# A query sketch sent through DRAM and read back repeated, later loads ungated: polysketch attention followed by a squared-ReLU feed-forward

## The chip, the cores and the metric

The kernel runs on 1 core of one Trainium2 chip. The metric is device microseconds of one execution; a kernel's number is the median of its runs. Engines in the profiles: PE (matmuls), PEld (its weight loads), DVE (vector), ACT (scalar), POOL (GpSimd), SP (issues most transfers).

## The reference

```python
def phi(x):                                   # S1, S2: 8 x 32;  x: (4 batches, 4 heads, 1088, 32)
    a = np.einsum('rd,bhsd->bhsr', S1, x)     # first sketch
    b = np.einsum('rd,bhsd->bhsr', S2, x)     # second sketch
    return np.einsum('bhsi,bhsj->bhsij', a, b).reshape(*x.shape[:-1], 64)
q_p, k_p = phi(q), phi(k)
kv = np.einsum('bhsf,bhsd->bhfd', k_p, v)
z = np.sum(k_p, axis=2)
num = np.einsum('bhsf,bhfd->bhsd', q_p, kv)
den = np.einsum('bhsf,bhf->bhs', q_p, z)[..., None] + 1e-06
x = (num / den) as (4352 tokens, 128)
r = np.maximum(x @ w_in, 0.0)                 # w_in: 128 x 2048
out = (r * r) @ w_out                         # w_out: 2048 x 128
```

The work falls into attention, batch by batch, and the feed-forward in chunks of 512 tokens, which needs the attention of its tokens.

## The kernel before

At build time a small list scheduler inside the kernel puts some 600 operations in a fixed order on each engine, from a table of ranks and its own guesses of durations. At run time each engine works through its list and waits on semaphores. So an engine doesn't overtake its own list, even when something behind is ready (in early_no_trip below, POOL stood for 15.9 us before one product, with copies behind it).

The query path of batches 1 to 3. PE makes both sketches in repeated form (64 rows for the 8 x 8 pairs: one repeats its rows, the other tiles them), ACT copies one out of PSUM, DVE multiplies it with the other:

```python
for u, (base, n, xs_) in enumerate(((0, 256, (0, 1)), (512, 256, (0, 1)), (1024, 64, (0,))) if b else ...):
    def f_m(e, ...):
        for ab in range(2):                    # both sketches
            for x in xs_:
                for h in range(H):
                    ...
                    nc.tensor.matmul(at(hb[x])[64 * y : 64 * y + 64, c0 : c0 + n],
                        SR[32 * h : 32 * h + 32, ab].rearrange("p x y -> p (x y)"), rhs, start=True, stop=True)
    def f_ac(e, ...):
        nc.scalar.copy(at(sA)[:, 0 : 2 * n]..., src(ab=0))
    def f_qp(e, ...):
        nc.vector.tensor_tensor(out=o, in0=i0, in1=i1, op=ALU.mult)      # qp
```

The loads. POOL issues weights and the inputs of batches 1 to 3 in one chain, paced by landings three transfers back. The first waits for v of batch 0, and the loads of batches 2 and 3 wait for the first normalised output of the batch before:

```python
o_gate = add("gate", {"POOL": ...}, lambda e: nc.gpsimd.tensor_copy(gate[96:128], vin[0][96:128, H - 1, 7, D - 1 : D]), ...)
...
load_v(1, -35)
load_q(1, -34)
...
if b > 1:
    load_k(b, vt(0) - 30, hist[(b, "gate")])
    load_v(b, vt(0) - 29)
    load_q(b, vt(0) - 28)
...
def f_gt(e, db=db):
    nc.gpsimd.tensor_copy(gateb, at(db)[2][:, 0, 0:1])      # waits for xs of batch b
```

The denominators get epsilon on DVE (`nc.vector.tensor_scalar_add(dn_, v4[:, :, :, D], eps)`), then reciprocal, product (`xs`), transpose on PE (`xT`), feed-forward.

## Time and profile before

| | before |
|---|---|
| median, range of its first 3 runs | 119.99 us, 119.92 to 120.73 |
| span of the profiled run, mean clock of PE | 118.0 us, 0.995 |
| first denominators of batches 0 and 1 | 12.81, 37.32 us |

Columns: line, engine, operation, out<-in, shapes, count | busy us, mean ns | idle time of the engine just before, and what ended most of it.

```profile
L707 ACT ACTIVATE r<-h 128x1024 bf16<-128x1024 f32 x53 | 52.0, 1046 | 4.6 <-PE h L698 3.3
L698 PE MATMUL h<-xT,w_in 128*128 128x512 bf16 (+1 forms) x152 | 36.2, 348 | 1.0 <-ACT r L707 0.7
...
L717 DVE TENSOR_TENSOR g<-r 128x1024 bf16<-128x1024 bf16 x46 | 30.6, 698 | 0.7 <-ACT r L707 0.3
L715 ACT ACTIVATE g<-r 128x1024 bf16<-128x1024 bf16 x22 | 23.7, 1089 | 0.2
L709 DVE TENSOR_SCALAR r<-h 128x1024 bf16<-128x1024 f32 x15 | 18.0, 1210 | 1.1 <-PE h L698 1.1
...
L629 PE MATMUL h<-kvz,qp 128*64 128x66 f32 x288 | 10.4, 225 | 0.4 <-DVE kvz L553 0.2
```

Relu (`r`) and square (`g`) of the feed-forward take 52.0 + 23.7 us of ACT and 30.6 + 18.0 of DVE, 124.3 us, so 62 us for each of the two engines. PE's own part of the feed-forward is 272 matmuls of 512 columns at 0.215 us, 58.5 us.

### The profile page before, as it was taken

The page shows a single profiled execution, that of the slowest core. Times are in us where ns is not written, and L with a number is a line of the kernel's source. Part 1 is how long each engine was busy: PE and PEld are TensorE (multiplying, and loading weights), DVE is VectorE, ACT ScalarE, POOL GpSimd, SP SyncE. Part 2 cuts the span into 40 slices and gives each one's busy share as a digit, 9 for nine tenths or more (in the row PEclk, how much of TensorE's full clock was granted, in tenths as well). Part 3 has the DMA queues.
Part 4 walks back from the last instruction along what each step waited for, and adds up shares of the span by engine and source line. Part 5 has one row for each costly group of instructions (what it writes and reads, how often), then busy time and mean ns, then how long its engine had stood idle before and what let it go on. Part 6 is the DMA issues. An engine that isn't in the chain of part 4 may idle for free.

```text
span 118.0 us, 3582 instructions
## 1 busy us (share of the span) xinstructions
PE 108.2 (92%) x1442; PEld 66.6 (56%) x1460; DVE 96.6 (82%) x179; ACT 91.9 (78%) x140; POOL 30.5 (26%) x73
## 2 busy tenths in 40 slices
PE   5998999999999998999999999999899999999850
PEld 2377676665666653555757545447656544567640
DVE  2658579989959699997559999999679989999920
ACT  0542367699885799999997999998649999999910
POOL 6139165593000764600006643300000000000000
PEclk9999999999999999999999999999999999999998
DMA  3960968774210299200401948102200050040522
GB/s 107 291 170 6 154 169 126 105 200 183 37 16 6 62 292 232 73 6 10 74 11 23 298 82 235 24 12 39 48 0 0 3 89 8 6 81 3 89 45 45
DMA packets 22272, 10.19 MB, mean 86 GB/s; under 512 B 19008, under 2 KB 20672, under 8 KB 22256
## 3 DMA queue, kind: packets, MB, share of 16 engines
q0 software_dynamic: 2688, 6.06, 20.6%
q1 hardware_dynamic: 18560, 3.54, 15.1%
q10 hardware_dynamic: 1008, 0.36, 1.4%
q8 instruction: 11, 0.18, 0.7%
q14 instruction: 5, 0.04, 0.1%
HBM read 8.78 MB, written 2.23 MB: 93 GB/s over the span
## 4 chain that ended last, share of the span: by engine, by line
PE 53%; ACT 18%; DVE 12%; issue 8%; DMA 4%; POOL 2%; DVEq 0%; ACTq 0%
PE o L724 16%; PE h L698 15%; ACT r L707 10%; PE h L629 6%; PE o L325 5%; DMA kin<-in_k_dram 4%; DVE g L717 4%; ACT g L715 3%; PE a L538 3%; PE h L583 2%; DVE qp L609 2%; PE a L496 2%; ACT A L598 2%; PE h L496 2%; DVE kT L476 1%
## 5 line engine op out<-in xcount | busy, mean ns | idle before, releaser
L707 ACT ACTIVATE r<-h 128x1024 bf16<-128x1024 f32 x53 | 52.0, 1046 | 4.6 <-PE h L698 3.3
L698 PE MATMUL h<-xT,w_in 128*128 128x512 bf16 (+1 forms) x152 | 36.2, 348 | 1.0 <-ACT r L707 0.7
L724 PE MATMUL o<-g,w_out 128*128 128x512 bf16 (+1 forms) x154 | 33.7, 346 | 1.5 <-DVE osb L731 0.5
L717 DVE TENSOR_TENSOR g<-r 128x1024 bf16<-128x1024 bf16 x46 | 30.6, 698 | 0.7 <-ACT r L707 0.3
L715 ACT ACTIVATE g<-r 128x1024 bf16<-128x1024 bf16 x22 | 23.7, 1089 | 0.2
L698 PEld LDWEIGHTS <-w_in 128*128 128x128 bf16 x160 | 16.6, 115 | 12.6 <-issue 3.1
L724 PEld LDWEIGHTS <-w_out 128*128 128x128 bf16 x160 | 15.1, 98 | 13.4 <-issue 1.6
L709 DVE TENSOR_SCALAR r<-h 128x1024 bf16<-128x1024 f32 x15 | 18.0, 1210 | 1.1 <-PE h L698 1.1
L609 DVE TENSOR_TENSOR qp<-h,A 128x512 f32<-128x512 f32 (+2 forms) x22 | 11.9, 562 | 2.9 <-ACT A L598 2.8
L598 ACT COPY A<-h 128x512 f32<-128x512 f32 (+2 forms) x22 | 10.0, 504 | 4.7 <-PE h L583 4.6
L629 PEld LDWEIGHTS h<-kvz,qp 128*64 128x64 f32 x288 | 9.2, 137 | 3.7 <-DVE qp L609 2.0
L583 PE MATMUL h<-qT,SR 32*64 32x256 f32 (+2 forms) x352 | 10.8, 338 | 0.1
L629 PE MATMUL h<-kvz,qp 128*64 128x66 f32 x288 | 10.4, 225 | 0.4 <-DVE kvz L553 0.2
L325 PE MATMUL o<-wz 128*128 128x512 bf16 x26 | 8.6, 450 | 1.5 <-DVE mk L288 1.2
L538 PEld LDWEIGHTS a<-vp,kp 128*64 128x64 f32 x216 | 6.9, 138 | 2.8 <-issue 2.2
L583 PEld LDWEIGHTS h<-qT,SR 32*64 32x64 f32 x352 | 6.2, 131 | 3.1 <-ACT r L707 0.8
L538 PE MATMUL a<-vp,kp 128*64 128x33 f32 x216 | 7.6, 224 | 0.2
L731 DVE STREAM_TRANSPOSE osb<-o 128x512 f32<-128x512 f32 (+1 forms) x10 | 6.3, 629 | 1.4 <-PE o L724 1.4
L663 POOL COPY gateb<-xs 128x1 bf16<-128x1 bf16 x3 | 0.6, 189 | 25.3 <-DVE xs L652 25.3
L360 POOL DMA_DIRECT2D vin<-in_v_dram x12 | 6.6, 560 | 0.4 <-issue 0.4
L476 DVE STREAM_TRANSPOSE kT<-kin 128x512 f32<-128x512 f32 x8 | 5.3, 681 | 1.4 <-DMA kin<-in_k_dram 1.4
L521 DVE TENSOR_TENSOR kp<-a,ka 128x512 f32<-128x512 f32 (+1 forms) x8 | 5.9, 747 | 0.5 <-ACT kb L511 0.5
(65 smaller groups left out, 88.5 us busy)
## 6 DMA issues: line engine op xcount, KB each, us to landing
kin<-in_k_dram POOLq DMA_DIRECT2D x3, 544.0 KB, 5.1
qin<-in_q_dram POOLq DMA_DIRECT2D x3, 544.0 KB, 3.6
vin<-in_v_dram POOLq DMA_DIRECT2D x12, 128.0 KB, 4.5
out_dram<-osb SPq DMA_DIRECT2D x16, 64.0 KB, 1.9
w_in<-in_moe_w_in_dram POOLq DMA_DIRECT2D x4, 128.0 KB, 3.7
w_out<-in_moe_w_out_dram POOLq DMA_DIRECT2D x4, 128.0 KB, 3.9
qin<-in_q_dram SPq DMA_DIRECT2D x1, 416.0 KB
out_dram<-osb SPq DMA_DIRECT2D x10, 32.0 KB, 1.6
```

The source lines that it names most:

```text
L325: nc.tensor.matmul(tiles["o"][0][:, 0:512], wz[:, 0:128], wz, start=True, stop=True)
L538: nc.tensor.matmul(t[64 * (h % 2) : 64 * (h % 2) + 64, 33 * (h // 2) : 33 * (h // 2) + 33], kp[i][:, j, h, :], vp[i][:, h, j, :], start=(j ...
L583: nc.tensor.matmul(at(hb[x])[64 * y : 64 * y + 64, c0 : c0 + n], SR[32 * h : 32 * h + 32, ab].rearrange("p x y -> p (x y)"), rhs, start=Tr ...
L598: nc.scalar.copy(at(sA)[:, 0 : 2 * n].rearrange("p (r s) -> p r s", s=n), src(ab=0))
L609: nc.vector.tensor_tensor(out=o, in0=i0, in1=i1, op=ALU.mult)
L629: nc.tensor.matmul(at(nb)[64 * hf : 64 * hf + 64, col(x, pr)], qp[i][:, pr, n0 : n0 + 64], kvz[i][xx % 2][:, pr].rearrange("p y d -> p (y ...
L698: nc.tensor.matmul(at(hb)[:, step * w : step * w + N], w_in[:, 512 * (ct // E) : 512 * (ct // E) + 512].rearrange("p (c e) -> p e c", e=E) ...
L707: nc.scalar.activation(o, view(at(hb)), ACTF.Relu)
L709: nc.vector.tensor_scalar_max(o, view(at(hb)), 0.0)
L715: nc.scalar.activation(at(gb)[:, 0 : W * N], r, ACTF.Square)
L717: nc.vector.tensor_tensor(out=at(gb)[:, 0 : W * N], in0=r, in1=r, op=ALU.mult)
L724: nc.tensor.matmul(at(ob)[:, 0:N], w_out[:, ct, :], at(gb)[:, N * w : N * w + N], start=(ct == 0), stop=(ct == CT - 1))
```

## The change

The intent: take the repetition of one sketch off PE, and its copy off ACT. For batches 1 to 3, PE makes this sketch A compact (32 output rows a group), A is written to DRAM, and two transfers read it back repeated eight times into SBUF. The other sketch is made in tiles of 512 columns and multiplied by A from SBUF. The first gate goes from v to the first part of q of batch 0; batch 1's q is loaded ahead of its v; the loads of batches 2 and 3 have no gate of their own. Epsilon is added on ACT, key products are cut differently, and the order on all engines is new.

```diff
-        for u, (base, n, xs_) in enumerate(
-                ((0, 256, (0, 1)), (512, 256, (0, 1)), (1024, 64, (0,))) if b else ...
+        if b:
+            def f_A(e):
+                w = lambda x: SKD[:, x].rearrange("p r y c -> p (r y c)")
+                for g in range(4):
+                    nc.tensor.matmul(at(ab_)[32 * g : 32 * g + 32, 0:256], w(g // 2), qT[i][:, 256 * g : 256 * g + 256], ...)
+                ...
+            o_As = add(f"As{b}", {"ACT": act(272), "DVE": dve(272)}, ...)
+            o_aw = add(f"aw{b}", {"SP": (0.6, 3.0)}, lambda e: nc.sync.dma_start(
+                out=Aw[i].rearrange("r y j (g s) -> g (r y j) s", g=4), in_=As[i]), ...)
+            for pr in range(2):
+                def f_ar(e, pr=pr):
+                    nc.sync.dma_start(out=Ar[i][:, pr, :], in_=Aw[i][pr].rearrange("y j s -> (y j) s")[:, None, :].to_broadcast([16, R, S]))
+            def f_m(e):
+                ...                                  # one sketch, 8 matmuls of 512 columns
+            for x in range(2):
+                ...                                  # DVE: qp = sketch (PSUM) * Ar (SBUF), 1024 elements
...
-    o_gate = add("gate", ..., nc.gpsimd.tensor_copy(gate[96:128], vin[0][96:128, H - 1, 7, D - 1 : D]), ...)
+    o_gate = add("gate", ..., nc.gpsimd.tensor_copy(gate[96:128], qin[0][96:128, 0:1]), pri=-45)
...
-    load_v(1, -35)
-    load_q(1, -34)
+    load_q(1, -35)
+    load_v(1, -34)
...
-                load_k(b, vt(0) - 30, hist[(b, "gate")])
-                load_v(b, vt(0) - 29)
-                load_q(b, vt(0) - 28)
+                load_q(b, vt(0) - 30)
+                load_k(b, vt(0) - 29)
+                load_v(b, vt(0) - 28)
...
-                nc.vector.tensor_scalar_add(dn_, v4[:, :, :, D], eps)
+                    nc.scalar.activation(dn_, v4[:, :, :, D], ACTF.Identity, bias=epsT[:, 0:1])
```

## The prediction

> **What bounds the kernel now.** I read the page's busy table and slices first, then its chain that ended last, then the groups by line, and then the timeline in three places: the start, the query path of batch 1, and one later batch. The page of the kernel before gives, per engine, busy time, share of the span and instructions, and below it the busy tenths in 40 slices of 2.95 us:
>
> ```profile
> PE 108.2 (92%) x1442; PEld 66.6 (56%) x1460; DVE 96.6 (82%) x179; ACT 91.9 (78%) x140; POOL 30.5 (26%) x73
> ...
> PE   5998999999999998999999999999899999999850
> ...
> DVE  2658579989959699997559999999679989999920
> ACT  0542367699885799999997999998649999999910
> ...
> PE 53%; ACT 18%; DVE 12%; issue 8%; DMA 4%; POOL 2%; DVEq 0%; ACTq 0%
> ```
>
> The reader should see three engines near full, PE first, and PE as over half of the chain. DVE and ACT dip together in the first seven slices and near slices 12 to 14, 20 to 22 and 29 to 31. The last three dips are the query parts of batches 1 to 3. The groups concerned (busy us, mean ns of one):
>
> ```profile
> L724 PE MATMUL o<-g,w_out 128*128 128x512 bf16 (+1 forms) x154 | 33.7, 346 | 1.5 <-DVE osb L731 0.5
> ...
> L609 DVE TENSOR_TENSOR qp<-h,A 128x512 f32<-128x512 f32 (+2 forms) x22 | 11.9, 562 | 2.9 <-ACT A L598 2.8
> L598 ACT COPY A<-h 128x512 f32<-128x512 f32 (+2 forms) x22 | 10.0, 504 | 4.7 <-PE h L583 4.6
> ...
> L583 PE MATMUL h<-qT,SR 32*64 32x256 f32 (+2 forms) x352 | 10.8, 338 | 0.1
> ...
> L663 POOL COPY gateb<-xs 128x1 bf16<-128x1 bf16 x3 | 0.6, 189 | 25.3 <-DVE xs L652 25.3
> ```
>
> L583 makes both sketches of q, L598 copies one out of PSUM, L609 multiplies them: 4.6 us of ACT and 2.8 us of DVE go in waiting inside this hand-over. The gate's 25.3 us of POOL cost nothing by themselves, since POOL is 26% busy.
>
> Is PE really the bound? The timeline puts the first numerator's denominators of batches 1, 2 and 3 at 37.32, 61.72 and 85.68 us: a batch takes about 24.2 us. Four feed-forward matmuls of 512 columns take 0.86 us on the chain, so 0.215 each; a batch has 1088/512 x 32 = 68 of them, 14.6 us. Attention of batch 3, from the timeline: kv 1.13 + 1.36, key sketch 0.45 + 0.75 + 0.45, query sketch 1.12 + 1.12 + 0.46, numerator 1.16 + 1.39, transposes 0.39 + 0.52, in all 10.3 us, of which I estimate 1 us as overlap of pipeline ends with the next group. So PE has about 24 us of work in a 24.2 us batch: once running, it is bound by PE, with ACT and DVE some 10% short of full (between 40 and 66 us they were busy 24.27 and 21.83 of 26).
>
> The start is different. Until 40 us only 768 tokens (48 big-matmul equivalents of 512 columns, 10.3 us) and two attentions (some 19 us) are done. The lines of the start, from the timeline (start us, us, engine, what):
>
> ```profile
> 10.21 0.18 POOL L346 COPY gate<-vin 32x1 f32<-32x1 f32 x1
> ...
> 11.63 0.55 POOL L360 DMA_DIRECT2D kin<-in_k_dram  x1
> ...
> 25.20 0.56 POOL L360 DMA_DIRECT2D qin<-in_q_dram  x1
> ```
>
> Batch 1's keys are asked for at 11.6 us and used at 16.72, its queries asked for at 25.2 and used at 30.4, its last query product ends at 39.2. Meanwhile PE runs warm-up matmuls on zeros: 2.8 us of them after 15 us. So the start is bound by loads that are gated late.
>
> **What the Trainium skill says.** "TensorE: Matmul & The Clock Gate", section "Wait — 56ns, not 53.3ns?", gives 215.7 ns from start to start at N = 512 when warm; this trace's 0.215 us agrees, so nothing is to be had from the feed-forward matmuls. "TensorEngine Tiling (Array Packing)", "Key Properties": changing the tiling mode drains TensorE; the trace shows 0.38 to 0.42 us of idle weight loading ahead of most L583 and L538 groups. One group more per batch (A) and one fewer (a second L583) leave that about even. "ScalarE: Activation LUTs", "What ACT_TABLE_LOAD costs": an ACTIVATE is 186 ns + 0.833 ns per element, 93 ns more for each pointer operand, and neighbours overlap by 93 ns. A copy of 512 should be 613 ns; the trace has 607. "DMA: Bandwidth & Descriptors", "Why a DMA increments its semaphore by 16 and not by 1": the number of DMA engines is the largest up to 16 that divides the slowest dimension of both sides. The write of the compact sketch has 4 as its slowest dimension in DRAM, so I estimate that it runs on 4 engines; its landing will show it.
>
> **The change part by part**, for each of batches 1 to 3.
>
> PE: the two full sketch groups (1.12 + 1.12 us; each 16 matmuls of 256 columns) become one of 8 matmuls of 512, the same 4096 columns, so 1.12 us. The tail goes from 0.46 to about 0.35. Added are 8 small matmuls of 32 output rows for A, which I put at 0.65 from the key sketch's 0.69 for 8. So 2.70 becomes 2.12: -0.6 a batch, **-1.8 us in all**, on the binding engine.
>
> ACT: 12 copies of 512 (7.8 us for 14, so 0.56 each, 6.7) and 3 of 128 (0.8) go: -7.5. Merged key copies: -0.6. Added: 12 adds of epsilon with a pointer bias, 186 + 13 + 93 - 93 = about 0.2 each, +2.4; one copy of 272, +0.4. About **-5.3**, before the different shares of v copies.
>
> DVE: 12 adds go (1.1 + 0.5 = 1.6). Four products of 512 (0.66 busy each) become two of 1024: 1.042 ns per element plus 0.12 gives 1.19, so -0.3 a batch, -1.0. Two copies of 272 come, +0.9, and by the engine table some +0.4 of key products. About **-1.3**. With PE at its limit the 6.6 us of ACT and DVE are slack, not time; they only make the relu and square come sooner. I count 0.4 us for that.
>
> PSUM: of three big buffers, a pair was held twice a batch, through sketch, ACT copy and DVE product. Now a pair is held once, and only through sketch and product, because the sketch waits for A's repeat. That shortens the stretch in which the feed-forward has one buffer left; I count 0.3 us a batch at most, 0.5 in all.
>
> DMA: per batch 139 KB are written and 2 x 557 KB read back. Loads of 544 KB land in 3.6 to 5.1 us and stores of 64 KB in 1.9. I estimate 3 for the write on few engines and 5 to 6 for the pair, so 8 to 9 us from A's copy to the product. The traffic grows by (139 + 1114) x 3 = 3.8 MB on 10.19, from a share of about 37% to 50%. A batch is 24 us long, and q is loaded first and no longer gated, so for batches 2 and 3 this lies beside other work.
>
> The start: the gate moves from v (10.2 us) to the first part of q, whose 128 KB landed 4.0 us after their issue at 1.64, so near 6. The chain of loads, paced by landings three back, moves up by about 4 us, and q comes before v: batch 1's q by about 21 instead of 29. Its A round trip takes 8 to 9 of those 8 back, and A's product then stands at about 30 to 34, against 33.7 to 39.2 before. The feed-forward's third chunk can start 3 to 4 us sooner; half of that is real, as PE then is nearer full and v of batch 0 shares the DMA engines. I count **-2 us**.
>
> Sum: -1.8 - 0.4 - 0.5 - 2.0 = -4.7, less 0.2 for contention: 120.0 - 4.5 = **115.5 us**.
>
> **Rivals.** (1) The round trip becomes the wait. The product needs both read backs; they share SP's queue with stores, which already waited 83.7 us on DVE, and a store standing ahead of a read holds it. If A comes 3 us late in each batch, PE runs out of feed-forward work, xT comes late, and some 2 us a batch return: 119 to 121. For it: everything depends on one order fixed beforehand. Against it: the loads are ungated and a batch has 24 us to hide 9. (2) Everything is hidden anyway and only PE's 1.8 us count, because the start is bound by batch 0's own chain (kv to numerator to xT, 14.4 us) and not by the gate: about 118. For it: the first feed-forward matmul at 15.4 us waits for both. Against it: the queries at 30.4 us. (3) DVE becomes the bound, as 1024-element products hold it 1.2 us at a time, and squares wait behind: +0.5 us a batch, 117. (4) Early weight loads collide with v of batch 0: the first numerator slips by 1 us.
>
> **Range and chances.** The certain part (PE) gives 118.2; all parts at full size, with all of the 4 us at the start, give 112.8. A failed round trip gives 120 or more. I take 115.5 with 112.8 to 118.2. Faster by over 2% means below 117.6: 0.76; within 2%: 0.20; slower: 0.04, as runs agree to 0.7%.
>
> **What would show it.** PE: L583's successor at half its former 10.8 us or somewhat more, and A's group near 0.65 us. ACT: no A copies, busy some 5 us less. Write landing near 3 us, reads 4 to 6, and the product's wait on the read back under 1 us in batches 2 and 3. The gate near 6 us, batch 1's q issued before 18 us, batch 1's first denominators near 34 instead of 37.3. If later batches still take 24.2 us each, the PE step is wrong; if the first denominators stay at 37, the step on the start is wrong; if PE waits under L583's successor on a DMA, rival 1 holds.

## The result and the profile after

The changed kernel is right and takes 125.91 us in the median (124.66 to 126.89), against 120.18 for the kernel before on the same chip. The ratio is 1.039, 95% interval 1.031 to 1.047: slower by 4%. Ratios here are the mean time of one kernel's fast runs over that of the other's fast runs of the same rounds, so they are not quite the ratio of the medians that are quoted. Two of the four runs (126.57 and 126.89) count as slow; the two fast ones are 124.66 and 125.26. The profiled one is the 124.66, with a span of 122.9 us and a mean clock of 0.981.

The page of the changed kernel, its busy table and three rows of its slices (40 slices, now 3.07 us each):

```profile
PE 111.2 (91%) x1340; PEld 67.3 (55%) x1340; DVE 99.2 (81%) x162; ACT 86.8 (71%) x138; POOL 27.9 (23%) x69
...
ACT  0434265899864000499999969999979998999910
...
PEclk9999999999999995899999999999999999999997
DMA  4979587666699999970014960040031040040422
```

ACT has a hole of three empty slices, from 40 to 49 us. From 34 us to past its end, at 52, the DMA engines are full (six nines), and in the hole's last slice the clock granted to PE falls to half of full speed. The chain that ended last and two groups, from the same page:

```profile
PE 55%; ACT 14%; DMA 11%; DVE 9%; issue 7%; SPq 0%; DVEq 0%; ACTq 0%
...
L740 ACT ACTIVATE den<-h,epsT 128x16 f32<-128x16 f32 (+1 forms) x8 | 2.2, 278 | 10.5 <-PE h L719 10.3
L632 DVE TENSOR_TENSOR qp<-h,Ar 128x1024 f32<-128x1024 f32 x6 | 7.2, 1218 | 2.3 <-DMA Ar<-Aw 2.1
```

DMA is now 11% of the chain (4% before). The pieces of the chain between 29.9 and 50 us say which transfers (start us, us, what):

```profile
29.95 5.36 DMA Aw<-As
...
35.97 8.07 DMA Ar<-Aw
...
45.65 1.30 PE h L719 x32
46.94 0.80 PE a L566 x16
47.74 2.25 PE h L719 x40
```

The write of A takes 5.36 us and the read back 8.07. That is the round trip of batch 1, alone on the chain. From the timeline of the changed kernel:

```profile
6.83 0.19 POOL L369 COPY gate<-qin 32x1 f32<-32x1 f32 x1
...
20.07 0.53 POOL L385 DMA_DIRECT2D qin<-in_q_dram  x1 [0.30 <-issue]
...
40.76 1.11 PE L624 MATMUL h<-qT,SR 32*64 32x512 f32 x16
...
44.17 1.23 DVE L632 TENSOR_TENSOR qp<-h,Ar 128x1024 f32<-128x1024 f32 x1 [2.06 <-DMA Ar<-Aw]
...
46.98 0.27 ACT L740 ACTIVATE den<-h,epsT 128x16 f32<-128x16 f32 x1 [7.55 <-PE h L719]
```

The gate opens 3.4 us sooner than before and batch 1's q is asked for 5.1 us sooner (25.20 before). The sketch, L583's successor L624, takes 1.11 us for a batch as expected, where L583 took 1.12 + 1.12. (PE's busy time rose all the same, from 108.2 to 111.2 us: the warm-up matmuls took 9.7 instead of 8.6, and a stretch at a lower clock added some 1.5, see section 1.) But the first product of batch 1 stands at 44.17, and its first denominators come at 46.98 us, 9.7 us later than before (37.32). DVE waited for the read back in batch 1 alone: the group above has 2.1 us of it, and 2.06 of these are this one wait.

### The profile page after: what moved, and what is told of

The parts are those of the page before. It is cut to its first block, busy times and chain, and to the rows that moved or that the text cites.

```text
span 122.9 us, 3359 instructions
## 1 busy us (share of the span) xinstructions
PE 111.2 (91%) x1340; PEld 67.3 (55%) x1340; DVE 99.2 (81%) x162; ACT 86.8 (71%) x138; POOL 27.9 (23%) x69
## 4 chain that ended last, share of the span: by engine, by line
PE 55%; ACT 14%; DMA 11%; DVE 9%; issue 7%; SPq 0%; DVEq 0%; ACTq 0%
PE o L813 13%; PE h L787 13%; ACT r L796 8%; PE h L719 7%; PE o L347 7%; DMA Ar<-Aw 7%; ACT g L804 5%; DMA Aw<-As 4%; DVE r L798 3%; PE a L566 3%; PE h L673 3%; PE a L521 2%; DVE g L806 2%; PE h L566 2%; DVE qp L632 2%
## 5 line engine op out<-in xcount | busy, mean ns | idle before, releaser
L796 ACT ACTIVATE r<-h 128x1024 bf16<-128x1024 f32 x49 | 47.6, 1035 | 4.5 <-PE h L787 4.2
L813 PE MATMUL o<-g,w_out 128*128 128x512 bf16 (+1 forms) x160 | 34.7, 347 | 1.9 <-DVE g L806 0.9
L798 DVE TENSOR_SCALAR r<-h 128x1024 bf16<-128x1024 f32 x19 | 23.1, 1215 | 2.4 <-PE h L787 1.8
L719 PE MATMUL h<-kvz,qp 128*64 128x66 f32 x272 | 10.9, 240 | 2.7 <-DVE qp L650 2.6
L719 PEld LDWEIGHTS h<-kvz,qp 128*64 128x64 f32 x272 | 9.8, 151 | 4.1 <-DVE qp L650 2.7
L347 PE MATMUL o<-wz 128*128 128x512 bf16 x30 | 9.7, 456 | 1.2 <-DVE mk L303 1.2
L740 ACT ACTIVATE den<-h,epsT 128x16 f32<-128x16 f32 (+1 forms) x8 | 2.2, 278 | 10.5 <-PE h L719 10.3
L546 POOL TENSOR_TENSOR kp<-kb,ka 128x768 f32<-128x768 f32 x2 | 3.6, 1808 | 25.9 <-issue 21.4
L632 DVE TENSOR_TENSOR qp<-h,Ar 128x1024 f32<-128x1024 f32 x6 | 7.2, 1218 | 2.3 <-DMA Ar<-Aw 2.1
L745 DVE TENSOR_TENSOR xs<-h,rec 128x512 bf16<-128x512 f32 (+1 forms) x8 | 5.4, 675 | 0.8
L546 DVE TENSOR_TENSOR kp<-a,ka 128x1024 f32<-128x1024 f32 (+2 forms) x6 | 5.9, 985 | 0.0
L590 DVE STREAM_TRANSPOSE qT<-qin 128x576 f32<-128x576 f32 (+3 forms) x8 | 5.7, 727 | 0.1
```

The source lines that it names most:

```text
L347: nc.tensor.matmul(tiles["o"][0][:, 0:512], wz[:, 0:128], wz, start=True, stop=True)
L546: (nc.gpsimd if e == "POOL" else nc.vector).tensor_tensor(out=kp[i][:, j0:j1].rearrange("p j h (x y) -> p (j h) x y", y=R), in0=bb[:, :, N ...
L632: nc.vector.tensor_tensor(out=qp[i][:, :, 512 * x : 512 * x + 512].rearrange("p r (g s) -> p r g s", g=2), in0=at(hb[x]).rearrange("p (r g ...
L719: nc.tensor.matmul(at(nb)[64 * hf : 64 * hf + 64, col(x, pr)], qp[i][:, pr, n0 : n0 + 64], kvz[i][(xx // 4 if b else xx) % 2][:, pr].rearr ...
L796: nc.scalar.activation(o, view(at(hb)), ACTF.Relu)
L798: nc.vector.tensor_scalar_max(o, view(at(hb)), 0.0)
```

## The experiments

Eighteen kernels ran. Except where said, each keeps the order of every engine of the kernel that it is made from: the scheduler is replaced by the order that it had made, written out, so that an edit doesn't move anything else. "Wrong on purpose" means that the output isn't the reference's, which is accepted for a measurement of time.

| run | what | median us | ratio to before, 95% interval |
|---|---|---|---|
| no_trip | changed, no round trip | 120.75 | 1.001 [0.997, 1.005] |
| no_late_loads | changed, no loads for batches 2 and 3 | 120.82 | 1.002 [0.997, 1.008] |
| aw16 | changed, write laid out on all DMA engines | 123.12 | 1.019 [1.014, 1.024] |
| gate_v | changed, first gate on v again | 126.55 | 1.045 [1.039, 1.052] |
| q3_late | changed, batch 3's loads held | 125.92 | 1.046 [1.040, 1.051] |
| hot | changed, PE kept busy in the hole | 124.41 | 1.030 [1.024, 1.036] |
| fix | changed, four writes and batch 3's loads held | 125.12 | 1.037 [1.031, 1.042] |
| all_chip | no round trips, searched order | 120.74 | 1.000 [0.995, 1.006] |
| b1_chip | round trips of batches 2, 3 only, searched order | 121.00 | 0.990 [0.983, 0.998] |
| half_sketch | before, PE makes one sketch of two | 120.50 | 0.998 [0.996, 1.001] |
| half_no_copy | the same, and no copies on ACT | 119.58 | 0.993 [0.990, 0.995] |
| early_loads | before, with the change's start | 120.86 | 1.002 [0.999, 1.004] |

In b1_chip the ratio rests on its two fastest runs (118.98, 120.17), which alone count as fast, and leaves out the others (120.86 to 121.45), at a clock of 1.0 in the profiled one; its median, level with before, is the better number. Six more runs, of orders that did not work, are told at the end.

### 1. Take the round trip away: no_trip

```diff
-            o_aw = add(f"aw{b}", ...)                       # write A
-            ... o_ar.append(add(f"ar{b}.{pr}", ...))        # two read backs
-            Av = Ar[i].rearrange("p r (g s) -> p r g s", g=4)
+            Av = qT[i].rearrange("p (g s) -> p g s", g=4)[:, None].to_broadcast([128, 2, 4, 272])
```

> The changed kernel with its order on every engine replayed, but A neither written to DRAM nor read back; the product takes q transposed in place of A's repeat (wrong on purpose, same shapes and the same work on PE, ACT and DVE). Theory (batch 1's round trip is what is exposed): the first product of batch 1 no longer waits 2.1 us for the read back at 44.17 but starts when its sketch is done, near 42; the idle ACT stretch shrinks from 7.5 to about 5 us, the PE clock does not fall, and 2.5 to 4 us are won: 122 to 123.5. The rest of the loss would then be in the order, which had placed the sketch at 40.8 because it counted on a long trip. Rival (the trip is hidden, the new order and the shares of engines are simply slower): under 1 us won, 125 or more.

It took 120.75 us, so the round trips cost the changed kernel 3.8% by the ratios (1.039 and 1.001), about 4.6 us; between the profiled spans it is 4.0 (122.9 and 118.9). It won somewhat more than expected, and yet it only equals the kernel before. So the round trip explains the loss, but not why the gains are missing. Part of the difference is PE's clock. The chain of no_trip has the same three pieces as above:

```profile
43.29 1.16 PE h L736 x32
44.45 0.44 PE a L590 x16
44.89 1.20 PE h L736 x40
```

They take 2.80 us here and 4.35 in the changed kernel. The clock granted over 46 to 50 us was 0.57 there and 1.00 here, so about 1.5 us of the loss came after the trip, from matmuls at a lower clock.

### 2. Take the other transfers away: no_late_loads

The loads for batches 2 and 3 are dropped, and these batches compute from the data of batches 0 and 1. Its output is wrong, which doesn't matter for the time. The round trips stay.

```diff
-                load_q(b, vt(0) - 30)
-                load_k(b, vt(0) - 29)
-                load_v(b, vt(0) - 28)
+                for x in 'qkv':
+                    loads[b, x] = [None] * 5 if x == 'v' else None      # what lies in the buffers is used
```

> The changed kernel, same order, without the loads of batches 2 and 3 (they are computed from the data of batches 0 and 1: wrong on purpose). Theory (the loads that are no longer gated slow the trip): the write of batch 1's A lands in about 3.6 us instead of 5.4 and the read back in about 6.7 instead of 8.1, as in the quiet stretch of batch 3; batch 1's first denominators come about 3 us before 46.98, and the time falls to 122 to 123.5. Rival (the pair of reads fills the DMA engines by itself): read back still near 8 us, under 1 us won.

It took 120.82 us, the same as without any trip and less than expected. The timeline of the trip of batch 1:

```profile
29.40 0.69 SPq L631 DMA_DIRECT2D Aw<-As  x1
...
33.14 1.23 SPq L637 DMA_DIRECT2D Ar<-Aw  x2
...
41.48 1.19 DVE L655 TENSOR_TENSOR qp<-h,Ar 128x1024 f32<-128x1024 f32 x1
```

The write took 3.7 us to the issue of the read (5.4 with the loads), the read backs landed within 7.1 us of issue (8.1 with them), and the product shows no wait. So the trip of batch 1 takes about 11 us when no load is beside it (3.7 + 7.1, and some issue) and 14 beside the ungated loads (29.95 to 44.05), and with them gone the loss is gone too: it takes the trip and the loads together. The DMA engines were full from 35 to 40 us even here (share 0.92 to 1.05 in each of these microseconds): the read back fills them with no load beside it, only a few stores and the write of batch 2. A version with the trip and with the old gates for both later batches was not run; q3_late below comes nearest.

### 3. The write: aw16

```diff
-    Aw = [dr.tile([2, 2, R, S], F32, ...)]
+    Aw = [dr.tile([128, 272], F32, ...)]                     # 128 rows outermost
-                out=Aw[i].rearrange("r y j (g s) -> g (r y j) s", g=4), in_=As[i])
+                out=Aw[i], in_=As[i])                        # wrong on purpose: the read takes other rows
```

> The changed kernel, same order and same bytes, but the DRAM copy of A is laid out 128 x 272 so that the write's slowest dimension is 128 and not 4 (A's rows then come back permuted: wrong on purpose). Theory (the write runs on 4 DMA engines): the write of batch 3, in a quiet stretch, lands in about 2.2 us instead of 3.6, that of batch 1 in about 4 instead of 5.4, and 0.5 to 1.5 us are won. Rival (the write's time is a fixed cost and waiting behind other packets): 3.4 us or more in the quiet stretch, nothing won.

123.12 us; by the ratios (1.039 and 1.019) that is 2.5 us less than the changed kernel, by the profiled spans 2.2. Its two pieces of the chain:

```profile
30.64 4.80 DMA Aw<-As
...
36.13 7.26 DMA Ar<-Aw
```

The write is 0.56 us shorter and the read back 0.81, so the product came at 43.51, only 0.66 sooner. The larger part of the gain, 1.55 us, is the clock: it was 1.00 over 42 to 50 us, so the three pieces above took 2.80 us as in no_trip. The layout of the write itself is a small part of the loss.

The theory about the engines did hold. In the quiet stretch of batch 3, from the write's issue to the issue of the read, the changed kernel takes 3.60 us (61.36 to 64.96) and aw16 1.80 (59.16 to 60.96). While the data moved, the 16 DMA engines were busy for a share of 0.23 to 0.27 in the changed kernel (62.6 to 64.2 us), which is 4 of 16, and for 0.82 to 0.96 in aw16 (60.0 to 60.4 us). So the prediction's estimate of 4 engines was right.

### 4. The gate: gate_v

```diff
-... nc.gpsimd.tensor_copy(gate[96:128], qin[0][96:128, 0:1])
+... nc.gpsimd.tensor_copy(gate[96:128], vin[0][96:128, H - 1, 7, D - 1 : D])
```

> The changed kernel, same order, but the first gate waits for the last quarter of v as before, not for the first part of q. Theory (early weight loads do not disturb the start; the later first feed-forward matmul, 17.2 against 15.4 us, is due to the new order of batch 0): the first feed-forward matmul stays within 0.4 us of 17.2 us, v's first copy on POOL comes 0.3 us earlier at most, and batch 1's q lands about 1 us later, so the time is the same or up to 1 us longer. Rival (the weights collide with v of batch 0): the first feed-forward matmul comes back to about 15.5 us and 1 us or more is won.

126.55 us. The early gate isn't to blame for the loss. Neither figure for the first feed-forward matmul was met (it came at 21.99 us). The run doesn't say what the early gate is worth, since in this order POOL's copies of v then stand behind the weights' issues, and batch 0's first denominators slipped to 18.53 us.

### 5. Two remedies within the changed order, and the clock: q3_late, fix, hot

q3_late puts batch 3's loads behind a POOL copy that waits for batch 1's read back.

```diff
+            if b == 1:
+                add("gateA", {"POOL": ...}, lambda e: nc.gpsimd.tensor_copy(gt2, Ar[i][0:1, :, S - 1]), o_ar, ...)
```

> The changed kernel's order, with one thing moved: batch 3's loads are issued only when batch 1's read back has landed (a small copy on POOL waits for it). Result right. Theory (the round trip of batch 1 is long because the ungated loads share the DMA engines with it): the read back of batch 1 lands in 6 to 7 us instead of 8.07, batch 1's first product stands 1 to 2 us earlier (near 42.5 to 43 instead of 44.17), and the kernel takes 124 us, -1.5 to -2. Less than without the late loads at all (-5), since batch 2's loads still lie beside the write. Rival (the clock of PE makes the loss, and the loads don't matter): no change, 125.5.

Missed. The product came 0.94 us sooner (43.23), but the time is 125.92. Batch 3's q now came late, DVE waited 2.18 us for it at 47.96, ahead of other work in its list, and PE's clock fell all the same (0.61 over 50 to 54 us). The wait had moved.

fix has this and writes A as four transfers of 32 rows.

```diff
-lambda e: nc.sync.dma_start(out=Aw[i].rearrange("r y j (g s) -> g (r y j) s", g=4), in_=As[i])
+lambda e: [nc.sync.dma_start(out=...[g], in_=As[i][32 * g : 32 * g + 32]) for g in range(4)]
```

> The changed kernel's order with the write made as 4 transfers of 32 rows each (their slowest dimension is then 32 in place of 4), and batch 3's loads held until batch 1's read back has landed. Result right. From the run with the write laid out on all engines (-2.8) and the expectation for the held loads (-1.5 to -2): write to landing 3.5 to 4.5 us instead of 5.36, first product near 41.5 to 42.5, 121 to 122 us, so near the kernel before and still far from the 115.5 predicted. If the trip isn't the reason, it stays near 125.

Missed, 125.12. The four issues took 2.67 us of SP, 0.67 each, so the read back was issued at 37.17 us, 6.7 after the write began (5.4 in the changed kernel). Its profile fell in a slow run (126.89 us), so only these issues are read from it.

hot puts 12 matmuls on zeros in front of batch 1's first numerators.

```diff
+    for n in range(12):
+        add(f"hot{n}", {"PE": ...}, lambda e: nc.tensor.matmul(tiles["o"][0][:, 0:512], wz[:, 0:128], wz, ...))
```

> The changed kernel's order, with 12 matmuls on zeros put on PE just before batch 1's first numerators, into a free PSUM bank: 2.6 us of work in the stretch in which PE waited 2.63 us for the product. Result right. If the fall of the granted clock to 0.68 to 0.75 after this wait costs time by itself, the numerators of 40 take 1.4 us instead of 2.46, and the kernel gains 1 to 2 us (124 us) though the trip is as long as before. If the clock is of no account (the later work had slack), it stays at 125 to 126.

124.41; against the changed kernel's 1.039 its 1.030 has an overlapping interval. Its profile fell in a slow run, in which the read back took 10.2 us and the clock fell nevertheless. Its three fast runs (123.73 to 124.79) have a mean clock of 0.992 to 0.994, the changed kernel's two (124.66 and 125.26) of 0.981 and 0.982. That fits the expected gain, but it has no profile and lies within the noise. So what the clock costs by itself is not settled; the 1.5 us of section 1 is read from the chains of two other runs.

### 6. Is PE's time worth what the prediction counts? half_sketch, half_no_copy

These start from the kernel before, in its own order, and only take work away. Their outputs are wrong, which doesn't matter for the times.

```diff
 half_sketch
-                for ab in range(2):
+                for ab in range(1 if b else 2):
...
-                    i0, i1 = src(ab=1), ...
+                    i0, i1 = src(ab=0 if b else 1), ...
 half_no_copy, in addition
-                o_ac = add(f"qa{b}.{u}.{x}", {"ACT": act(2 * n)}, f_ac, [o_m], ...)
+                o_ac = o_m if b else add(...)                 # second factor: qT
```

> The kernel before, its order kept on every engine, with one thing taken away: in batches 1 to 3 PE makes only one of the two sketches of q (matmuls of 256 columns halved, 160 fewer), and the product is that sketch with itself. Result wrong on purpose. PE has 1.35 us less to do in each of three batches (half of 1.12 + 1.12 + 0.46), 4.0 us in all; ACT, DVE, POOL and the loads do all that they did. It measures what PE's time in the query part is worth. My prediction's step (PE is the binding engine, so what it saves counts in full): 116.5 to 117.5, -3 to -4. Rival (in the query part PE waits for ACT and DVE or these have the relu work to do anyway, so PE's saving turns into waiting): 119 to 120.5.

120.50 us, ratio 0.998 [0.996, 1.001]. The groups of PE in half_sketch, to be held against those of the kernel before (L698, L724 and L583 there):

```profile
L724 PE MATMUL h<-xT,w_in 128*128 128x512 bf16 (+1 forms) x152 | 36.3, 347 | 1.8 <-ACT r L733 0.7
L750 PE MATMUL o<-g,w_out 128*128 128x512 bf16 (+1 forms) x155 | 33.9, 346 | 1.7 <-ACT g L741 0.7
...
L655 PE MATMUL h<-kvz,qp 128*64 128x66 f32 x288 | 10.4, 225 | 1.2 <-DVE kvz L579 0.7
...
L609 PE MATMUL h<-qT,SR 32*64 32x256 f32 (+2 forms) x232 | 8.2, 337 | 0.5 <-DVE qp L635 0.3
```

The sketch group fell from 10.8 us to 8.2, less than the 4.0 that I had written down: 2.6. The time fell by 0.2 us (ratios: between 0.5 us less and 0.1 more). The idle time of PE ahead of these four groups went from 3.0 us (1.0, 1.5, 0.4 and 0.1) to 5.2 (1.8, 1.7, 1.2 and 0.5), ended mostly by ACT's and DVE's results. Between 15 and 113 us PE was busy for 94.4 us before and for 91.9 here. What PE saved, it waited.

> As half_sketch, and in batches 1 to 3 ACT's 15 copies of a sketch out of PSUM are gone too (the product takes q transposed as its second operand). Result wrong on purpose. ACT has some 7.5 us less, PE 4.0 less: more than the change takes from either, with nothing added. By my prediction's steps: -4.0 for PE, -0.4 for slack and -0.5 for PSUM, 115.5 to 116. Rival (ACT and DVE bind as much as PE, so that both have to fall): half_sketch gives little and this one gives 3 us or more over it.

119.58 us, ratio 0.993 [0.990, 0.995]. Its busy table:

```profile
PE 106.4 (90%) x1323; PEld 64.6 (55%) x1340; DVE 96.2 (82%) x179; ACT 85.5 (73%) x125; POOL 30.2 (26%) x73
```

ACT's busy time fell from 91.9 to 85.5 us as well, and the time fell by 0.9 us. Neither of the two theories has its size: PE and ACT, even together, set little of the time in this order. DVE kept all its work (96.6 before, 96.2 here), and no run takes work from DVE alone, so whether DVE holds the others, or the fixed order with its waits, stays open. Taking 2.6 us from PE and 6.4 from ACT, with nothing given back, buys 0.9 us in the order of the kernel before.

### 7. Is the early start worth what the prediction counts? early_loads

The kernel before, right result, with the change's gate, and q of batch 1 ahead of its v.

```diff
-... gate[96:128], vin[0][96:128, H - 1, 7, D - 1 : D] ...
+... gate[96:128], qin[0][96:128, 0:1] ...
-    load_v(1, -35)
-    load_q(1, -34)
+    load_q(1, -35)
+    load_v(1, -34)
```

> The kernel before, right result, with the start's part of the change alone: the first gate waits for the first part of q in place of v, batch 1's q is loaded ahead of its v, the small copy for the second gate goes behind these loads; later loads stay gated, the order on all other engines is kept. My prediction counted -2 us for this (118). Rival (batch 0's own chain, DVE and PE set the start, and the order of batch 1's work is fixed further on): q asked for near 20 to 21 us instead of 25.2 and used no sooner, 120 to 121; if the early weights hold up v of batch 0, 121 to 122.

120.86 us, ratio 1.002 [0.999, 1.004]. Its timeline:

```profile
6.21 0.18 POOL L372 COPY gate<-qin 32x1 f32<-32x1 f32 x1 [2.78 <-DMA qin<-in_q_dram]
...
16.19 0.60 PE L724 MATMUL h<-xT,w_in 128*128 128x256 bf16 x4
...
20.71 0.53 POOL L386 DMA_DIRECT2D qin<-in_q_dram  x1 [0.30 <-issue]
...
38.64 0.17 DVE L673 TENSOR_SCALAR den<-h 128x16 f32<-128x16 f32 x1
```

Batch 1's q is asked for 4.5 us sooner than before, and its first denominators come no sooner: 38.64 against 37.32. DVE takes q in hand at 31.89 us where it did so at 30.37, in the order that it keeps, and the v of batch 1 is now issued 1.2 us later (23.55 against 22.33). The first feed-forward matmul is 0.75 us later (15.44 before), and the first copy of batch 0's v on ACT starts at 8.22 us instead of 7.78. That isn't the early weights for certain: half_no_copy, with the old gate, has these two at 16.30 and 8.24. The order of the other engines was kept, so this says what the early loads do alone, not what the best order could make of them.

### 8. Other orders: all_chip, b1_chip, and six that did not work

all_chip has no round trip in any batch (every batch makes both sketches on PE), with the rest of the change; b1_chip has the trips of batches 2 and 3 only. Both are right, with an order searched over ranks in the kernel's own scheduler.

```diff
 b1_chip
-        if b:
+        if b > 1:                                            # all_chip: b > 9, never
             ab_ = Buf("a", "h")
```

> The change for batches 2 and 3 only: batch 1 makes both sketches of q on PE as the kernel before does (sketch, copy on ACT, product), so no round trip stands in the start; the early first gate, the ungated loads and the adds on ACT stay. A new order, found by a search over ranks in the kernel's own scheduling model (114.5 there, where the changed kernel's is 117.0). Result right. Theory (the round trip of batch 1 and the order planned around it are the whole loss; batches 2 and 3 gain by theirs): first denominators of batch 1 at 34 to 38 us instead of 46.98, span 116 to 117.5, time 118 to 119.5, faster than before by 1 to 2%. Rival (the ungated loads and the round trips of batches 2 and 3 cost as well): 121 to 124.

> The rest of the change without any round trip: all batches make both sketches on PE; the early first gate, the ungated loads and the adds of epsilon on ACT stay. Again a searched order (117.1 in the scheduling model). Result right. It tells what the DRAM path of batches 2 and 3 is worth against the run before it: my prediction put PE's saving at 0.6 us a batch plus 0.3 for slack and PSUM, so all_chip should be 1.5 to 2 us slower than b1_chip, 120 to 121; if the DRAM path gives nothing where there is time for it, the two are equal.

121.00 and 120.74 us: in the median level with each other and with the kernel before. The theory's 118 to 119.5 for b1_chip is missed in the median (in the profile, of a run of 121.13 us that counts as slow, the denominators came at 41.39 us, not by 38). The trips of batches 2 and 3 bring nothing that stands out from the noise, though there the product doesn't wait for them; and as the two programs also have different orders, the pair doesn't weigh the trips by themselves.

Two orders made by hand are void as experiments. early_no_trip (128.56 us, 125.63 to 129.41) placed a key product on POOL ahead of batch 2's v copies; it waited for a late key sketch and blocked POOL for 15.9 us. b1_early (134.49 us) gave a wrong result; I suspect that the order handed a buffer to a new tile ahead of its last reader, which no run shows.

> As the run without the trip (A neither written nor read back, the product takes q transposed instead; result wrong on purpose), but with the order of 30 to 47 us changed by hand: batch 1's query sketch, products, numerators and transposes stand ahead of batch 2's q and k transposes, key sketch and key products, which the changed kernel's order puts first on DVE and PE to fill the time of the trip. The run without the trip came out at the time of the kernel before (120.75) though PE had 1.8 us less to do; its chain between 24 and 43 us is DVE. Theory (the order made for the trip costs the rest: some 5 us of batch 2's DVE work stand before batch 1's products): first product of batch 1 near 34 to 37 us instead of 41.85, first denominators 37 to 39.5 instead of 44.49, 117 to 119 us. Rival (DVE is full in this stretch whatever the order, and batch 2's work comes back later): 120 to 121.

> The same order by hand with a right result: batch 1 makes both sketches of q on PE as the kernel before does, batches 2 and 3 go through DRAM, the early gate, the ungated loads and the adds on ACT stay. Against the run with a searched order (121.0, level with before) only the order differs. Theory: first denominators of batch 1 near 36 to 39, 118.5 to 120, so 0.5 to 1.5% faster than before, with two thirds of PE's saving left. Rival: 120.5 to 122.

Four more orders came from a search over single moves, timed in the scheduler's model with longer transfers.

> The whole change, right result, with a new order: a search that moves single instructions within a fixed order, timed in the kernel's scheduling model with all large transfers 1.25 times as long as it had them (so set, the model gives spans of 121.1, 119.3 and 119.1 us for the changed kernel, no_trip and b1_chip; the chip had 122.9, 118.9 and 119.4). It found 119.8 from 121.1. Theory (what is left of the loss after no_trip is the order, but batch 1's round trip in the start can't be hidden by any order, since there isn't other work enough before it): span 119 to 121, time 121 to 123, still slower than before. Rival (the order alone was bad): 118 or less.

> As no_trip (A neither written nor read back, result wrong on purpose), with an order searched in the same way for just this program: 116.2 in the model where no_trip's order has 119.3. Theory (no_trip came out level with before because it kept the order made for a 13 us trip): span 116 to 117.5, time 118 to 119.5, 1 to 2% faster than before. Rival (batch 2's work on DVE must be done somewhere, order is nothing): 120.5 to 121.5, as no_trip.

> Batch 1 on chip as in the kernel before, batches 2 and 3 through DRAM, all else as changed, right result, order searched in the same way: 115.5 in the model where b1_chip's order has 119.1. Theory: span 115.5 to 117, time 117.5 to 119, 1.5 to 2.5% faster than before: the best of both. Rival (the round trips of batches 2 and 3 and the ungated loads cost what PE saves): 120 to 121.

> No round trip at all, every batch makes both sketches on PE, all else as changed, right result, order searched in the same way: 116.8 in the model where all_chip's order has 120.1. Against re_b1_chip it tells what the DRAM path of batches 2 and 3 is worth: the prediction's 0.6 us of PE and 0.3 of slack and PSUM a batch say 1.8 us, the model 1.3. Expected: span 116.8 to 118, time 118.5 to 120. If it equals re_b1_chip, the DRAM path is worth nothing even where it is hidden.

Measured: re_change 130.43 (ratio 1.070), re_no_trip 122.94 (1.019), re_b1_chip 122.46 (1.015), re_all_chip 122.26 us (1.015). All missed; each is slower than the order that it came from. In re_no_trip the first denominators of batches 0 and 1 came at 15.33 and 46.66 us, later than in no_trip (14.48 and 44.49). That the search had used up the model's errors in the start is likely and not shown. So no version beats the kernel before by a margin that I would claim, and whether some order would is open. The pair re_b1_chip and re_all_chip is once more level (0.2 us apart), as b1_chip and all_chip were.

## Why the prediction was wrong

Predicted 115.5 us, measured 125.9, outside the range of 112.8 to 118.2; faster was given 0.76, and it is slower. Two steps failed: that PE's saving counts in full, which took the gain away, and that the round trip is hidden, which made the loss. By its own steps:

- **PE, -1.8 us "on the binding engine".** The work did shrink as said: the sketch takes 1.11 us a batch and A's group 0.69 (28.66 to 29.35 us in batch 1), where 0.65 was estimated. That it would count in full is the step that failed first. half_sketch took 2.6 us from the same PE group in the kernel before and won 0.2 (between 0.5 less and 0.1 more). The prediction read 92% busy and 53% of the chain as "bound by PE" and called ACT and DVE's share slack. It compared PE's work with a batch's length, but never summed relu and square: 62 us for each of ACT and DVE, beside 58.5 for PE's feed-forward. So, as I read it, the engines bind in turn, and what one saves it spends waiting for the others; that DVE alone holds the others is not excluded. The prediction's own sign, "if later batches still take 24.2 us each", would have passed the step: from denominators to denominators they took 23.1 and 18.7 us. The sign was a bad one, since the new order moves feed-forward work across it: 34.2 us follow batch 3's first denominators, and 32.3 did before.
- **ACT and DVE slack, -0.4, and PSUM, -0.5.** half_no_copy won 0.9 us in all with more taken away from PE and ACT than the change takes. ACT fell by 5.1 us where 5.3 was predicted, but luck has a part in it: relu and square fell from 75.7 to 71.9 us of ACT because the new order gives DVE four relus more (19 for 15, at 1.2 us), while the adds of epsilon took 3.3 us and not 2.4, and ACT makes more of the copies of v and kvz. For the same reason DVE rose by 2.6 instead of falling by 1.3 (whose products, by the prediction's own figures, sum to -0.8 and not -1.0). In the changed kernel none of this shows in the time. The reason given for PSUM was wrong: the sketch does not wait for A's repeat. It reads only q, and in batch 1 it ran at 40.76 us, 3.3 us before the repeat landed at 44.05. In the changed order its two halves and its tail hold all three big buffers, and they hold them while DVE waits for the transfer.
- **The start, -2.0.** The gate opened at 6.83 us, near 6 as predicted, but q was issued at 20.07 and not before 18, and landed near 26 us (the copy that waits for it starts at 26.33), not 21. Above all the sum took half of a gain in landing time for a gain in time. early_loads asks for q 4.5 us sooner and is 0.2 us slower, within its interval: so, at least in the order of the kernel before, the start was not bound by its loads, as the prediction had read it.
- **The round trip, "8 to 9 us from A's copy to the product", hidden.** This is the term that turned a lack of gain into a loss. It was 14.2 us from the write's issue to the product: 5.4 for a write estimated at 3, 8.1 for a pair of reads estimated at 5 to 6, the rest issue and the start of DVE. Alone it still takes 11. The estimate took the landing times of single loads from a profile in which the DMA engines were 37% busy, for a time in which the change itself fills them. In batch 1, where the prediction set it against an earlier q, there was not enough other work to hide it, and PE's clock fell after the hole.
- **Contention, +0.2.** Together with the exposed trip and the clock it is 4 to 5 us (no_trip and no_late_loads).

Rival 1 of the prediction, the round trip as the wait, is what happened, with 119 to 121 us as its price. The price was too low because the other gains were counted, and the place was another: not every batch, but batch 1, once. Rival 2, only PE's 1.8 us count, is refuted by half_sketch in the order of the kernel before. Rival 3, DVE as the bound with products of 1.2 us, was not tested by itself; the products do take 1.22 us. Rival 4, early weights in the way of v, isn't shown: early_loads has the first feed-forward matmul 0.75 us later, but half_no_copy, with the old gate, 0.86. The check "if PE waits on a DMA" would have missed it: it was DVE that waited for the transfer, and PE waited for DVE.

The measured terms, which come from different orders and need not add up, come close: no gain from PE, at most 0.9 from PE and ACT together, none from the start, 4 to 5 lost by the trip, so 123 to 125 from 120; the two fast runs took 124.66 and 125.26. What stays open is how much of the missing gain is the order. no_trip has the changed order without its trip and is level with the kernel before. Between 26 and 43 us its chain runs largely over DVE, where batch 2's transposes and key products stand ahead of batch 1's product, and that looks like an order made for a wait; but no better one was found.

## What to carry to other kernels

Before counting a saving on the busiest engine in full, take that work away in the kernel as it is, and see what the time does; and sum the work of the other engines in the same stage. A transfer that replaces work of an engine has to be priced at the load that the DMA engines will have then, its own included, and at the first place where it is used, where there may be nothing yet to hide it. Removing gates from loads is not free when a transfer on the critical path shares the same engines: here the write and the read back took 5.4 and 8.1 us beside the loads, 3.7 and 7.1 without.

## What the Trainium skill lacked or had wrong

- "DMA: Bandwidth & Descriptors", "Bandwidth", gives 341 GB/s for a load of 1 MB. The read back here, 2 x 544 KB in which each row of DRAM is read eight times, moved 161 to 283 GB/s in each of the microseconds from 35 to 40 with the engines full and no load beside it (no_late_loads; a few stores and the next batch's write were), and landed in up to 7.1 us. I found no figure there for a read that repeats its source.
- "TensorE: Matmul & The Clock Gate", "What's actually happening", has the clock fall to half after at least one idle window of about 3.4 us. In the changed kernel PE was idle for 2.63 us ahead of L719, and the granted clock over the next 4 us was 0.57; the numerators took 2.25 us instead of 1.20. In q3_late a gap of 2.15 us was followed by a clock of 0.50 from 51 to 54 us; after gaps of 1.28 (aw16) and 1.13 us (gate_v) it stayed at 1.00. So a gap shorter than a window was enough here.
- I found on no page what a round trip through DRAM costs as a whole, write, wait and read: about 11 us alone and 14 beside other loads for 136 KB written and 1.1 MB read.
